# Attention with expert routing on one core: a new order of the first steps, the early gathers, expert 2's weights and the x stores

## The chip, the cores and the metric

The kernel runs on one core of one Trainium2 chip. The metric is the device time of one execution in microseconds (us); lower is better. The engines of the core work from queues of their own: TensorE (PE, its weight loads are PEld), VectorE (DVE), ScalarE (ACT), GpSimd (POOL) and SyncE (SP). POOL and SP, and in one place ACT, also issue the transfers (DMA).

## The reference

Attention over 8 batches of 8 heads, 576 rows of 64, with a causal mask in blocks of 64; then each of the 4608 rows of 512 goes through the expert that its domain id names.

```python
# _attn_ref(q, k, v): B, H, S, D = 8, 8, 576, 64
scores = (1.0 / np.sqrt(D)) * np.matmul(q, k.transpose(0, 1, 3, 2))
mask = block_i >= block_j                    # blocks of 64 rows
attn = softmax(np.where(mask, scores, -1e9))
x = (attn @ v).transpose(0, 2, 1, 3).reshape(B * S, H * D)   # 4608 x 512

# _moe_ref(x, domain_id, w1, w2): E = 8, w1 is E x 512 x 1024, w2 is E x 1024 x 512
for e in range(E):
    mask = domain_id == e
    h = np.maximum(x[mask] @ w1[e], 0.0)
    out[mask] = h @ w2[e]
```

## The kernel before

**Attention.** The work is cut into 32 steps (`npair`), four per batch; a step takes two heads. Each step `p` of the main loop (line 532) works on two pairs, and every engine takes its instructions in the order in which the loop writes them; no scheduler moves them.

- `emit_G0`, `emit_G1` and `emit_G2` (lines 384 to 405) form the scores of a pair on PE, in PSUM tiles `ps` (two buffers), and ACT takes their exponential into `A`: three exponentials of 128 x 1024 per pair.
- `emit_P` and `emit_D` multiply the previous pair's `A` by its `v` into `po`; `emit_N` lets DVE divide by the sums and write 16-bit rows into `x`.
- `emit_T(G, s)` lets PE transpose q (s = 0) or k (s = 1) of two pairs, group G, through the one PSUM tile `PT`, and DVE copies it to `QK`. The table `Ts` and `turn_qk` say at which point of which step this happens: (step, 0) at the start, (step, 1) behind `emit_G2`, (step, 2) behind the next pair's `G0`.
- `routing()` is a generator that works out, on DVE and with a few small matmuls (line 290), which row goes to which slot of which expert. Each step takes one portion of it (`next(rout, None)`), and step 24 takes the rest with `inv_mm` and `inv_close`, after which the table of row numbers `tok0` is known.

**Loads and stores.** POOL issues all loads: q, k and v of the batches in four buffers each (`qh`, `kh`, `vS`), a batch's v in five pieces by 128 rows, and the experts' weights in halves of w1 and w2 (`w1_half`, `w2_half`), which are converted from 32 to 16 bits on the way. A POOL transfer takes one of eight semaphores in turn, and so waits until the transfer eight before it has landed. `store_x` writes the normalised rows to the DRAM tensor `x_rows`: a small part (64 rows) and a large one (512 rows) per batch, for the last batch in two column parts, 0 to 320 behind step 31 and 320 to 512 behind step 32. SP issues them, but for the last large one, which ACT issues (line 449, `eng`).

**Experts.** Each expert has five blocks of 128 slots. A block's rows come from `x_rows` by an indirect transfer (a gather, line 468). The first three blocks of experts 0 and 1 hold rows of batches 0 to 4 only, so their gathers (`early_gather`, line 497, with a copy of the row numbers by `early_row`) are issued during the attention; the late ones (lines 679 to 682) wait for the last x store. `early_block` has PE transpose expert 0's first three blocks in steps 30 and 31. For the others DVE transposes (`turn`, line 618, 16 instructions), except blocks 3 and 4 of experts 0 and 1, which go through PE (`transpose_block`). `mm1` (line 635) forms the first product, ACT takes the positive part (line 639); `mm2` (line 648) forms the second, ACT copies it (line 654), and POOL scatters it to the output (line 655). Experts 0 and 1 are run in two parts: three early blocks of each, then two late blocks of each. The lists `todo` say between which scatters the next weight halves are issued.

**What sets the order around the change.** In steps 26 to 31 line 590 holds a written list: a number is a half of the weights of experts 1 and 2 (0 to 7), a negative number an early gather of expert 1. Weights 4 and 5, expert 2's w1, are issued in the last two steps, ahead of the late gathers; weights 6 and 7 lie between the first scatters.

## Time and profile before

| | us |
|---|---|
| three timed executions | 280.13, 285.47, 284.68 |
| their median | 284.68 |
| profiled execution, own time | 279.41 |
| profiled execution, span | 277.6 |

The span is what the profile covers, from the first instruction to the last; the execution's own time is 1.8 us longer. Busy time in the span: PE 248.0 us (89%), DVE 187.3 (67%), ACT 164.7 (59%), POOL 158.1 (57%). Such shares are averages over stages with different limits; what limits a stage is read from the waits in it. "[1.02 <-ACT hT L639]" behind a row of a timeline means that the engine sat idle for 1.02 us before it, and that the instruction of line 639 on ACT ended this. DMA share is the busy time of the core's 16 transfer engines; it can exceed 1, as packets overlap.

### The profile page before, as it was taken

The numbers are of one execution on the slowest core, as the hardware profiler recorded it, in microseconds if no ns is written. First come the engines' busy times: TensorE is split into PE (matmuls) and PEld (weight loads), VectorE is DVE, ScalarE is ACT, GpSimd is POOL, SyncE is SP. The second block draws the span as 40 slices with busy tenths as digits, with TensorE's granted clock in tenths as the row PEclk, the third lists the DMA queues.
The fourth block names the chain that finished last, engine by engine and source line by source line (L and its number), as shares of the span: only waits on it lengthen the run. The fifth ranks groups of instructions, "written<-read, shape, count | busy, mean of one in ns | idle before, by whom it ended". The sixth has DMA issues, their size and how long they took to land.

```text
span 277.6 us, 6942 instructions
## 1 busy us (share of the span) xinstructions
PE 248.0 (89%) x2878; PEld 154.9 (56%) x2878; DVE 187.3 (67%) x297; ACT 164.7 (59%) x218; POOL 158.1 (57%) x184
## 2 busy tenths in 40 slices
PE   8599799999999998891899989999999999999940
PEld 5366566666667665550456656474664656647510
DVE  4769899999997783329139919899495983960000
ACT  1658989999997899450335545364452644536420
POOL 8797473554635544305784888687778875151240
PEclk9989999999999999998699999999999999999985
DMA  6999999999999999994379989999899994121030
GB/s 86 158 153 176 222 192 209 197 212 189 224 194 213 196 231 253 243 239 98 103 162 239 258 234 198 271 186 259 193 223 275 192 266 173 63 109 61 38 135 2
DMA packets 65585, 50.85 MB, mean 183 GB/s; under 512 B 40973, under 2 KB 53773, under 8 KB 65552
## 3 DMA queue, kind: packets, MB, share of 16 engines
q0 software_dynamic: 59936, 45.63, 95.8%
q1 hardware_dynamic: 5088, 4.56, 6.1%
q8 instruction: 24, 0.39, 0.5%
q10 hardware_dynamic: 528, 0.20, 0.3%
q14 instruction: 9, 0.07, 0.1%
HBM read 67.15 MB, written 15.20 MB: 297 GB/s over the span
## 4 chain that ended last, share of the span: by engine, by line
PE 40%; DMA 19%; issue 15%; POOL 13%; DVE 4%; another core or an unknown queue 3%; ACT 2%; POOLq 1%; DVEq 0%; ACTq 0%
PE ps L373 8%; PE ph L635 7%; PE po L415 7%; DMA kh<-in_k_dram 7%; DMA out_dram<-osb,tok 7%; PE po L648 7%; POOL out_dram L655 5%; PE PT L362 5%; DMA xg<-x_rows,row 4%; PE po L426 4%; DVE xT L618 3%; POOL vS L94 2%; POOL xg L468 2%; PE ps L395 1%
## 5 line engine op out<-in xcount | busy, mean ns | idle before, releaser
L618 DVE STREAM_TRANSPOSE xT<-xg 32x640 f16<-32x640 f16 (+1 forms) x112 | 89.4, 798 | 28.5 <-DMA xg<-x_rows,tok 13.4
L378 ACT ACTIVATE A<-ps 128x1024 f16<-128x1024 f32 x96 | 92.1, 1024 | 13.1 <-PE ps L395 6.4
L635 PE MATMUL ph<-xT,w1h 128*128 128x320 f16 (+2 forms) x512 | 74.6, 303 | 9.3 <-DVE xT L618 6.9
L648 PE MATMUL po<-w2h,hT 128*128 128x512 f16 x320 | 71.2, 379 | 0.1
L639 ACT ACTIVATE hT<-ph 128x640 f16<-128x640 f32 (+2 forms) x80 | 47.5, 597 | 37.2 <-PE ph L635 29.6
L635 PEld LDWEIGHTS <-w1h 128*128 128x128 f16 x512 | 50.4, 99 | 33.4 <-issue 14.1
L655 POOL DMA_INDIRECT out_dram<-osb,tok x40 | 40.6, 1015 | 37.9 <-ACT osb L654 25.1
L648 PEld LDWEIGHTS <-hT 128*128 128x128 f16 x320 | 31.2, 98 | 36.1 <-issue 0.6
L654 ACT COPY osb<-po 128x512 f32<-128x512 f32 x40 | 23.4, 586 | 46.7 <-PE po L648 30.7
L468 POOL DMA_INDIRECT xg<-x_rows,tok x34 | 34.5, 1016 | 23.9 <-DMA x_rows<-x 13.3
L94 POOL DMA_DIRECT2D vS<-in_v_dram x40 | 33.2, 837 | 23.9 <-DMA kh<-in_k_dram 10.0
L365 DVE COPY QK<-PT 128x1152 f16<-128x1152 f16 x30 | 40.5, 1350 | 3.4 <-PE PT L362 2.4
L373 PE MATMUL ps<-QK 64*128 64x64 f16 (+3 forms) x320 | 39.2, 296 | 2.4 <-ACT A L378 0.8
L415 PE MATMUL po<-vS,A 128*128 128x65 f16 x640 | 29.8, 197 | 1.1 <-issue 0.4
L415 PEld LDWEIGHTS <-A 128*128 128x128 f16 x640 | 23.6, 99 | 10.4 <-issue 7.0
L439 DVE TENSOR_TENSOR x<-po,rc 128x640 f16<-128x640 f32 x32 | 26.4, 824 | 1.1
L426 PE MATMUL po<-vS,A 64*64 64x65 f16 (+1 forms) x320 | 21.0, 194 | 0.0
L373 PEld LDWEIGHTS <-QK 64*128 64x128 f16 x320 | 13.2, 94 | 7.4 <-issue 1.3
L426 PEld LDWEIGHTS <-A 64*64 64x64 f16 (+1 forms) x320 | 14.2, 106 | 1.9
L128 POOL DMA_DIRECT2D w2h<-in_moe_w_dram x16 | 12.2, 767 | 3.5 <-DMA kh<-in_k_dram 2.3
L123 POOL DMA_DIRECT2D w1h<-in_moe_w_dram x16 | 12.2, 767 | 3.2 <-DMA qh<-in_q_dram 1.9
L438 DVE RECIPROCAL rc<-po 128x10 f32<-128x10 f32 x32 | 7.0, 220 | 10.1 <-PE po L426 8.2
(102 smaller groups left out, 126.6 us busy)
## 6 DMA issues: line engine op xcount, KB each, us to landing
w1h<-in_moe_w_dram POOLq DMA_DIRECT2D x16, 512.0 KB
w2h<-in_moe_w_dram POOLq DMA_DIRECT2D x16, 512.0 KB
vS<-in_v_dram POOLq DMA_DIRECT2D x28, 128.0 KB
x_rows<-x SPq DMA_DIRECT2D x7, 512.0 KB, 9.6
qh<-in_q_dram POOLq DMA_DIRECT2D x6, 576.0 KB
kh<-in_k_dram POOLq DMA_DIRECT2D x6, 576.0 KB
vS<-in_v_dram POOLq DMA_DIRECT2D x16, 64.0 KB
qh<-in_q_dram POOLq DMA_DIRECT2D x3, 288.0 KB
```

Source lines behind the costliest of these rows:

```text
L94: nc.gpsimd.dma_start(out=vS[b % RV][r0:128, c, h0:h1, 16:80], in_=v[b, h0:h1, 128 * c : 128 * c + n, :].rearrange("h p d -> p h d"))
L365: nc.vector.tensor_copy(out=QKs[G][:, s].rearrange("p i (n j) -> p i n j", j=R), in_=P16.rearrange("p (j i n) -> p i n j", j=R, i=2))
L373: nc.tensor.matmul(out=o[:, t], lhsT=QK[h, 1, i, 128 * c : 128 * c + 128], rhs=QK[h, 0, i, q0:q1], start=True, stop=True)
L378: nc.scalar.activation(out=o, in_=i, func=AF.Exp, scale=0.125)
L415: nc.tensor.matmul(out=po[:, t, 65 * w : 65 * w + 65], lhsT=st["A"][:, t, n0 : n0 + 128], rhs=vS[b % RV][:, c, head(st, t), 15:80], start= ...
L426: nc.tensor.matmul(out=po[r0:128, t, 65 * w : 65 * w + 65], lhsT=st["A"][k : k + 64, t, n0 : n0 + 128 - r0], rhs=vS[b % RV][k : k + 64, c, ...
L468: nc.gpsimd.indirect_dma_start(out=g[:, blk, :], out_offset=None, in_=xd, in_offset=bass.IndirectOffsetOnAxis(ap=tok[:, 1, blk : blk + 1], ...
L618: nc.vector.transpose(out=dst[32 * j : 32 * j + 32, i, b0:b1], in_=src[32 * i : 32 * i + 32, j, b0:b1])
L635: nc.tensor.matmul(out=ph[:, i, 0:w], lhsT=w1_cols(w1h, dc, fc), rhs=xT[:, dc, c0 : c0 + w], start=(dc == 0), stop=(dc == 3))
L639: nc.scalar.activation(out=hT[:, fc, n0 : n0 + k * w].rearrange("p (i n) -> p i n", i=k), in_=ph[:, 0:k, 0:w], func=AF.Relu)
L648: nc.tensor.matmul(out=po[:], lhsT=hT[:, fc, 128 * blk : 128 * blk + 128], rhs=w2h[:, fc, :], start=(fc == 0), stop=(fc == 7))
L655: nc.gpsimd.indirect_dma_start(out=dst[blk], out_offset=bass.IndirectOffsetOnAxis(ap=tok[:, 0, blk : blk + 1], axis=0), in_=osb[:], in_off ...
```

## The change

It has five parts.

1. The early gathers of expert 1 are issued in the middle of steps 25, 26 and 27 (`mid_issue`), among those of expert 0, and stand ahead of expert 1's weights but for one half of w1. `early_row` becomes part of `early_gather`.
2. Weights in the loop are those of experts 0 and 1 alone (`late_issue`); expert 2's w1 is issued behind the late gathers of experts 0 and 1, ahead of expert 2's gathers.
3. `store_x` always uses SP, and the large part goes first.
4. In steps 0 and 1 the scores `G1` stand ahead of `turn_qk(p, 0)`; in step 2 the transpose of `turn_qk(2, 1)` stands behind the next pair's `G0`; the portion of the routing stands behind `turn_qk(p, 2)`.
5. Batch 1's first k load follows its first q load directly, and batch 1's v comes in ten pieces (four heads each) in place of five.

```diff
-    load_qk(1, 0, 2, (0,))
+    load_qk(1, 0, 2)
     load_v_chunks(0, 4, H, range(4))
-    load_qk(1, 0, 2, (1,))
     load_qk(1, 2, HP)
-    load_v_chunks(1, 0, H, range(5))
+    for h0 in (0, HP):
+        load_v_chunks(1, h0, h0 + HP, range(5))
...
-    def store_x(st, c0, c1, eng):
+    def store_x(st, c0, c1):
         b = st["p"] // HP
         x = st["x"]
-        nc.sync.dma_start(out=xd[S * b : S * b + 64, c0:c1], in_=x[64:128, 4, c0:c1])
-        eng.dma_start(
+        nc.sync.dma_start(
             out=xd[S * b + 64 : S * b + S, c0:c1].rearrange("(m p) d -> p m d", p=128),
             in_=x[:, 0:4, c0:c1])
+        nc.sync.dma_start(out=xd[S * b : S * b + 64, c0:c1], in_=x[64:128, 4, c0:c1])
...
+    mid_issue = {25: ((1, 0),), 26: ((1, 1),), 27: ((1, 2),)}
+    late_issue = {22: (0, 0), 24: ((0, 0), 0), 25: (0, (0, 1)), 26: (0, (0, 2)),
+                  27: (0,), 28: (0,), 29: (0,)}
...
-        turn_qk(p, 0)
         if p <= 1:
             emit_G1(st)
+        turn_qk(p, 0)
...
             emit_N(prev)
+            for g in mid_issue.get(p, ()):
+                early_gather(*g)
...
             emit_G2(st)
-            turn_qk(p, 1)
+            if p != 2:
+                turn_qk(p, 1)
...
+        if p == 2:
+            turn_qk(p, 1)
+        turn_qk(p, 2)
         next(rout, None)
-        turn_qk(p, 2)
...
-        for g in ((0,), (1, -1, 2), (-2, 3), (-3,), (4,), (5,))[p - 26] if 26 <= p < npair else ():
-            if g < 0:
-                early_gather(1, -1 - g)
+        for g in late_issue.get(p, ()):
+            if isinstance(g, int):
+                todo.pop(0)()
             else:
-                todo[g]()
+                early_gather(*g)
...
     for e in range(2):
         gather(xgs[e], tok_of(e), range(NE, NB))
+    todo = weights(2)
+    for f in todo[0:2]:
+        f()
     xgs[2] = new_xg()
     gather(xgs[2], tok_of(2), range(NB))
...
-    mm2(hT0, w2s[0], tok_of(0), dst_of(0), range(NE), todo[6:8])
+    mm2(hT0, w2s[0], tok_of(0), dst_of(0), range(NE), todo[2:4])
```

POOL's order from expert 0's third early gather to expert 2's gathers, before. `xg_2203` is expert 0's buffer, `xg_2204` expert 1's, `xg_2760` expert 2's; `w1h_2364` and `w2h_2365` are expert 1's weights, `w1h_2366` is expert 2's; `row02` is the row numbers of expert 0's third block.

```order
L499 DMA xg_2203<-x_rows,row02_2359 128x512
L123 DMA w1h_2364<-in_moe_w1_dram 128x2x1024 x2
L499 DMA xg_2204<-x_rows,row10_2368 128x512
L128 DMA w2h_2365<-in_moe_w2_dram 128x2x1024
L499 DMA xg_2204<-x_rows,row11_2370 128x512
L128 DMA w2h_2365<-in_moe_w2_dram 128x2x1024
L499 DMA xg_2204<-x_rows,row12_2372 128x512
L123 DMA w1h_2366<-in_moe_w1_dram 128x2x1024 x2
L468 DMA xg_2203<-x_rows,tok0_140 128x512 x2
L468 DMA xg_2204<-x_rows,tok0_140 128x512 x2
L468 DMA xg_2760<-x_rows,tok0_140 128x512 x5
```

The same stretch of POOL's order in the changed kernel: `xg_2174`, `xg_2175` and `xg_2765` are the buffers of experts 0, 1 and 2, `w1h_2209` and `w2h_2210` expert 1's weights, `w1h_2761` expert 2's.

```order
L494 DMA xg_2174<-x_rows,row01_2295 128x512
L494 DMA xg_2175<-x_rows,row11_2341 128x512
L123 DMA w1h_2209<-in_moe_w1_dram 128x2x1024
L494 DMA xg_2174<-x_rows,row02_2377 128x512
L494 DMA xg_2175<-x_rows,row12_2423 128x512
L123 DMA w1h_2209<-in_moe_w1_dram 128x2x1024
L128 DMA w2h_2210<-in_moe_w2_dram 128x2x1024 x2
L468 DMA xg_2174<-x_rows,tok0_145 128x512 x2
L468 DMA xg_2175<-x_rows,tok0_145 128x512 x2
L123 DMA w1h_2761<-in_moe_w1_dram 128x2x1024 x2
L468 DMA xg_2765<-x_rows,tok0_145 128x512 x5
```

Expert 1's three early gathers (`row10` two places ahead of this stretch, then `row11`, `row12`) moved ahead of its w2 and of the second half of its w1, expert 0's third one (`row02`) fell behind `row11` and half of w1, and expert 2's w1 moved behind the four late gathers.

ACT's order at the end of the attention, before: the last six exponentials (line 378), then the x store, then expert 0's first product.

```order
L378 ACTIVATE A_80<-ps 128x2x512 x3
L378 ACTIVATE A_81<-ps 128x2x512 x3
L449 DMA x_rows<-x 128x4x192
L639 ACTIVATE hT<-ph 128x384 x8
L654 COPY osb<-po 128x512 x3
```

The same place in the changed kernel (lines 636 and 651 are 639 and 654 of before).

```order
L378 ACTIVATE A_80<-ps 128x2x512 x3
L378 ACTIVATE A_81<-ps 128x2x512 x3
L636 ACTIVATE hT<-ph 128x384 x8
L651 COPY osb<-po 128x512 x3
L636 ACTIVATE hT<-ph 128x384 x8
```

The store left ACT's queue, so the positive part of expert 0's first product follows the last exponential directly.

DVE's order in steps 0 to 2, as a difference: line 365 is the copy of transposed q or k out of `PT`, lines 283 to 293 belong to the routing, lines 438 and 439 are `emit_N`.

```order
 L283 SCALAR_TENSOR_TENSOR inc<-msk,me 128x288
 L286 CAST mr<-inc 128x8
+L365 COPY QK<-PT 128x1152
 L291 COPY sc<-po 128x24
-L365 COPY QK<-PT 128x1152 x2
-L438 RECIPROCAL rc<-po 128x10
-L439 TENSOR_TENSOR x<-po,rc 128x2x5x64
+L365 COPY QK<-PT 128x1152
+L438 RECIPROCAL rc<-po 128x10
+L439 TENSOR_TENSOR x<-po,rc 128x2x5x64
+L365 COPY QK<-PT 128x1152
 L293 TENSOR_SCALAR off<-sc 128x8
```

The copies of transposed q and k moved ahead of the routing's portions: the first one ahead of line 291, the third one ahead of lines 293 to 302.

## Rows read from the trace of the kernel before

**Rows 1.** PE's timeline: start, busy us, instruction [idle before, what ended it].
```profile
116.40 4.24 PE L635 MATMUL ph<-xT,w1h 128*128 128x384 f16 x24 [1.02 <-ACT hT L639]
120.48 5.34 PE L648 MATMUL po<-w2h,hT 128*128 128x512 f16 x24
132.76 7.17 PE L635 MATMUL ph<-xT,w1h 128*128 128x384 f16 x32 [6.94 <-DVE xT L618]
...
179.74 8.85 PE L635 MATMUL ph<-xT,w1h 128*128 128x320 f16 x64
...
249.36 8.86 PE L635 MATMUL ph<-xT,w1h 128*128 128x320 f16 x64
```

**Rows 2.** Windows: length, busy us of each engine, PE clock, DMA share, GB/s.
```profile
115.00:120.00 5.00, 3.98 (x25) 2.14 (x23) 0.09 (x1) 2.84 (x6) 0.00 (x0) 1.00 1.11 242
...
126.00:128.00 2.00, 0.00 (x0) 0.00 (x0) 1.95 (x5) 0.44 (x1) 0.88 (x1) 1.00 0.46 88
...
130.00:135.00 5.00, 2.24 (x8) 1.09 (x9) 2.56 (x5) 0.49 (x1) 3.83 (x4) 0.50 0.35 105
...
145.00:150.00 5.00, 4.84 (x36) 3.32 (x35) 4.90 (x7) 2.84 (x8) 4.16 (x5) 1.00 1.05 253
...
155.00:160.00 5.00, 4.93 (x34) 3.23 (x34) 4.75 (x11) 2.71 (x8) 3.89 (x5) 1.00 1.09 263
```

**Rows 3.** DVE's timeline, end of attention and experts 1, 3 and 7.
```profile
114.26 0.82 DVE L439 TENSOR_TENSOR x<-po,rc 128x640 f16<-128x640 f32 x1
123.30 9.31 DVE L618 STREAM_TRANSPOSE xT<-xg 32x384 f16<-32x384 f16 x16 [8.22 <-DMA xg<-x_rows,row]
...
166.01 13.58 DVE L618 STREAM_TRANSPOSE xT<-xg 32x640 f16<-32x640 f16 x16 [5.38 <-PE ph L635]
...
233.76 13.58 DVE L618 STREAM_TRANSPOSE xT<-xg 32x640 f16<-32x640 f16 x16 [5.54 <-DMA xg<-x_rows,tok]
```

**Rows 4.** POOL's timeline, 111 to 163 us.
```profile
111.19 1.07 POOL L499 DMA_INDIRECT xg<-x_rows,row  x1 [0.30 <-issue]
112.27 1.57 POOL L123 DMA_DIRECT2D w1h<-in_moe_w_dram  x2
127.12 1.05 POOL L468 DMA_INDIRECT xg<-x_rows,tok  x1 [13.29 <-DMA x_rows<-x]
...
138.97 1.04 POOL L655 DMA_INDIRECT out_dram<-osb,tok  x1 [0.30 <-issue]
...
153.13 0.98 POOL L655 DMA_INDIRECT out_dram<-osb,tok  x1 [3.36 <-ACT osb L654]
...
162.60 1.00 POOL L468 DMA_INDIRECT xg<-x_rows,tok  x1 [0.30 <-issue]
```

**Rows 5.** Timeline of PE's weight loads, early blocks of expert 0.
```profile
108.64 0.23 PEld L482 LDWEIGHTS <-xg 128*128 128x128 f16 x4 [0.34 <-DMA xg<-x_rows,row]
...
112.16 0.21 PEld L482 LDWEIGHTS <-xg 128*128 128x128 f16 x3 [0.39 <-issue]
```

**Rows 6.** DMA issues: KB each, median us from issue to landing.
```profile
x_rows<-x SPq DMA_DIRECT2D x7, 64.0 KB, 5.5
x_rows<-x SPq DMA_DIRECT2D x1, 320.0 KB, 12.0
...
x_rows<-x ACTq DMA_DIRECT2D x1, 192.0 KB, 11.2
```

**Rows 7.** ACT's timeline, start of the attention.
```profile
15.60 1.02 ACT L378 ACTIVATE A<-ps 128x1024 f16<-128x1024 f32 x1 [3.32 <-PE ps L395]
```

**Rows 8.** PE's timeline, transposes of k.
```profile
13.65 1.17 PE L362 MATMUL PT<-identh,kh 128*64 128x128 f16 x18 [1.46 <-DVE QK L365]
...
34.44 0.69 PE L362 MATMUL PT<-identh,kh 128*64 128x128 f16 x18 [0.87 <-DMA kh<-in_k_dram]
```

**Rows 9.** POOL's timeline, loads of batches 1 and 2.
```profile
17.11 4.22 POOL L94 DMA_DIRECT2D vS<-in_v_dram  x5
...
22.04 0.79 POOL L75 DMA_DIRECT2D kh<-in_k_dram  x1
```

More of the change, by code (lines that the diff above doesn't have):

```diff
@@ L489, in early_block @@
                      xgs[0], xT, blk)
-    rows = {}
-    def early_row(e, w):
-        rows[e, w] = const.tile([128, 1], I32, name=f"row{e}{w}")
-        nc.vector.tensor_copy(out=rows[e, w][:], in_=tok_of(e)[:, 1, w : w + 1])
     def early_gather(e, w):
-        row = rows[e, w]
+        row = const.tile([128, 1], I32, name=f"row{e}{w}")
+        nc.vector.tensor_copy(out=row[:], in_=tok_of(e)[:, 1, w : w + 1])
         nc.gpsimd.indirect_dma_start(
@@ L555 @@
             emit_N(prev)
+            if p == 24:
+                xgs = {0: new_xg(), 1: new_xg()}
+                xT = new_xT()
+            for g in mid_issue.get(p, ()):
+                early_gather(*g)
             if prev["p"] == npair - 2:
-                store_x(prev, 0, DM - 192, nc.sync)
+                store_x(prev, 0, DM - 192)
             elif prev["p"] == npair - 1:
-                store_x(prev, DM - 192, DM, nc.scalar)
+                store_x(prev, DM - 192, DM)
             elif prev["p"] % HP == HP - 1:
-                store_x(prev, 0, DM, nc.sync)
+                store_x(prev, 0, DM)
         if st is not None:
             emit_G2(st)
-            turn_qk(p, 1)
+            if p != 2:
+                turn_qk(p, 1)
             if p >= npair - 2:
@@ L577 @@
         if p == 22:
-            for f in weights(0):
-                f()
+            todo = weights(0)
         if p == 24:
-            xgs = {0: new_xg(), 1: new_xg()}
-            xT = new_xT()
-        if 24 <= p < 24 + NE:
-            early_row(0, p - 24)
-            early_gather(0, p - 24)
-        if p == 26:
-            todo = weights(1) + weights(2)
-            for w in range(NE):
-                early_row(1, w)
-        for g in ((0,), (1, -1, 2), (-2, 3), (-3,), (4,), (5,))[p - 26] if 26 <= p < npair else ():
-            if g < 0:
-                early_gather(1, -1 - g)
+            todo += weights(1)
+        for g in late_issue.get(p, ()):
+            if isinstance(g, int):
+                todo.pop(0)()
             else:
-                todo[g]()
+                early_gather(*g)
         prev = st
```

## The prediction

> **What bounds the kernel now.** I read the windows first, then the timeline of TensorE (PE), and for each of its waits the timeline of the engine that ends it.
>
> Up to the last normalisation at 114.26 the attention runs [rows 3]; from 133 us on the experts run back to back. Between them lies the one large hole: PE ends expert 0's second product at 125.82 and idles 6.94 us until the transposes xT of expert 1 [rows 1]. Its granted clock is 0.50 in 130 to 135 [rows 2], so the 32 matmuls that follow take 7.17 us, where 24 of the same shape took 4.24, so 5.65 for 32: 1.5 us. With the 1.02 us that PE waited for ScalarE (ACT) at 116.40 [rows 1], whose queue held an x store until VectorE (DVE) had finished, the prize is at most 6.94 + 1.5 + 1.0 = 9.5 us.
>
> What ends the hole: DVE starts expert 1's 16 transposes at 123.30, after 8.22 us of waiting for a gather, and needs 9.31 us [rows 3]. That gather is the third early one of expert 1, issued by GpSimd (POOL) at 111.19 behind two halves of w2 [rows 4]. It lands 12 us after its issue because the queue is full: from 115 to 120 the DMA share is 1.11 at 242 GB/s. In 130 to 135 it is 0.35 at 105 GB/s, as POOL then only issues gathers, nine from 127.12 to 138.97, one per 1.3 us [rows 2, 4]. So the kernel is bound by transferred bytes up to about 126 us, by POOL's issue to about 139, by bytes again to about 165, and by PE after that.
>
> Behind the hole stands a second chain with no slack. POOL's late gathers start at 127.12, after 13.29 us of waiting for the last x store. In order on POOL follow five gathers of expert 2, eight scatters between six weight halves (the first at 138.97), and five gathers of expert 3, the last one at 162.60 [rows 4]. DVE's turn of expert 3 starts at 166.01 and takes 13.58 us [rows 3], to 179.59; PE comes for it at 179.74 [rows 1]. Expert 3 is the narrow place. For expert 7 there is room: its turn starts at 233.76 and ends at 247.34, PE comes at 249.36 [rows 1, 3].
>
> **The change part by part.**
> *Early gathers of expert 1 ahead of its weights.* The third one no longer stands behind w2. But expert 0's third gather, which PE transposes at 112.16 in the last attention step, now stands behind two gathers of expert 1 (0.13 MB each) and half of w1 (0.52 MB). Expert 0's first gather already came only just in time: LDWEIGHTS waited 0.34 us for it at 108.64 [rows 5]. The third follows 0.26 MB later, at about 109.8, and now another 0.79 MB later, 3.3 us at 242 GB/s: about 113.4. So PE stands about 1.3 us (bounds 0 and 4). Expert 1's third gather lands at about 114.5. With PE 1.3 us late the last normalisation, which ended at 115.08 [rows 3], ends at 116.4, and DVE turns expert 1 until 125.7. PE starts expert 0 at 115.2, has no ACT wait, and is through its two products 5.65 + 5.34 us later, at 126.2. No hole, no low clock: expert 1's first product ends at 131.9, not 139.9, and all that PE does behind it could come 8.0 us earlier, expert 3 at 171.7.
>
> *x stores by SP, the large part first.* This gives the 1.02 us just counted. The small part goes out behind it, which the landing of the large one hides.
>
> *Expert 2's w1 behind the late gathers.* Two halves of 0.52 MB leave the queue ahead of the last store: 1.05 MB at 242 GB/s are 4.4 us. The share of 126 to 128 is 0.46, between full and gathers alone [rows 2], so the queue ran dry at about 126.3, and now at about 121.9. The last store is issued at 116.4. Rows bound its landing: 5.5 us (median of the 64 KB stores) to 12.0 us (the 320 KB store) [rows 6], so 121.9 to 128.4. I take 122.5, just behind the dry queue, as the 192 KB store before (115.12 + 11.2 = 126.3) landed just there. POOL started 0.8 us after that, and starts now at 123.3, 3.8 us earlier. The two halves of w1 now cost POOL 1.57 + 0.3 us ahead of expert 2's gathers [rows 4], so the first scatter comes 13.7 us after the start, at 137.0 in place of 138.97. Expert 2's gathers are issued by 136.7, landed 2.4 us later, and turned at about 152.7; PE wants them one expert's pace of 17.4 us (179.74 to 249.36 for four) ahead of expert 3, at about 154.
>
> *The narrow place afterwards.* Up to expert 3's gathers POOL's work is the same. Its 3.36 us wait at 153.13 for a scatter's data goes, as PE is 8 us ahead; by POOL alone those gathers come 5.0 us earlier. But the bytes stay: shares are 1.05 in 145 to 150 and 1.09 in 155 to 160 [rows 2], the queue is full, and its work starts only 2.0 us earlier. So expert 3's turn comes 2.0 us (bytes) to 5.0 us (POOL) earlier. With shares above 1 I take 3.0, near the bytes: turn 163.0 to 176.6, PE at 176.7 in place of 179.74. PE, ready at 171.7, waits there 5 us: the hole moves from expert 1 to expert 3. Experts 4 to 7 keep their room, as the pace of 17.4 us is PE's.
>
> *Steps 0 to 2 and batch 1's loads.* ACT idles 3.32 us before its fifth exponential at 15.60 [rows 7], as PE transposes k of the next group at 13.65, behind a 1.46 us wait for DVE, ahead of the scores [rows 8]. With scores first it starts at about 12.9, 2.7 us ahead. But PE then waits for batch 2's k, which landed only at 34.4, 12.4 us after its issue at 22.04 [rows 8, 9]; that landing hangs on the bytes ahead of it, and these are the same. Ten v loads of half size in place of five (five took 4.22 us [rows 9]) put its issue at most 4.2 us later, behind a queue that is still several us deep; the landing moves by 0 to 1.5 us. Bounds: 2.7 us gained to 1.5 lost. I take nothing: the wait at 34.4 swallows the lead, and the late gathers follow the bytes anyway.
>
> Sum: 3.0 us, at the narrow place; the 9.5 us of the hole lie beside it. The profiled execution took 279.41 us (span 277.6, 1.8 around it), so 276.4. It is the lowest of the four times shown; these average 282.4, and the median of the three is 284.68. No row tells what separates them, so I set the forecast at the average: 279.4.
>
> **A rule against my value for the store.** The last stores landed 11.2 and 12.0 us after their issue, beside a full queue [rows 6]. The Trainium skill ("DMA: Bandwidth & Descriptors", section "Anatomy of one DMA") fits a transfer through the software queue as about 2.0 us plus bytes over 436 GB/s; for 192 KB that is an estimate of 2.5 us. By it the store lands at 118.9 and the first rival below holds in full. The rows speak against it as long as the queue is full, as it is at 116.4.
>
> **Rivals.**
> *A. The queue is no limit behind the attention.* Expert 3's gathers land 2.4 us after their last issue, as in the profile (163.6 to 166.0), and the store at its lower bound. For it: the share of 0.35 in 130 to 135, with room for all of w1. Against it: shares above 1 from 145 to 160. Time: 5.0 us by POOL, 0.6 by the store, and more if it lands sooner still, up to PE's 8.0: about 7 us, 275.4.
> *B. The lead of the start lives.* If batch 2's k lands by 31.7, the attention ends 2.7 us earlier. For it: batch 1's k is asked for earlier. Against it: the same bytes ahead of batch 2. 279.4 - 2.7 = 276.7.
> *C. Slower: the store keeps its 12.0 us.* Place: POOL's first late gather. Issued at 116.4 the store lands at 128.4, POOL starts at 129.2, and with the 1.87 us for w1 the first scatter is at 142.9, 3.9 us later than before; expert 3's turn starts 0.9 us (POOL) to 3.9 us (bytes) later. It decides from a landing at 124.5 on: from there the first scatter is later than before. For it: both large stores of this stretch took 11 us or more. Against it: 1.05 MB less stand in the queue. Time: 2.4 us on 282.4, 284.8.
> *D. The order does not do what it says.* If expert 1's third gather still lands after 117 (126.2 less the 9.31 us of DVE), a part of the hole stays; the narrow place hides the first 5 us of it. Beyond 122 nothing is gained: 282.4.
>
> **How the numbers follow.** Forecast 0.53, A 0.22, B 0.07, C 0.13, D 0.05. Range 273.5 to 286.0: below A by 2, as the lowest time shown is 3 under the average that it starts from; above C by 1, as the times shown reach 285.47. About 2% (5.6 us) is what a measurement of this kernel can tell from no change. Faster by more than that: most of A, and a little of B and of the forecast, 0.25. Slower by more: the far part of C, 0.08. Within: 0.67.
>
> **What would show it.** Right: no PE wait before expert 1's first product and a clock of 1.00 there; POOL's first late gather at 122 to 125; a PE wait of 3 to 7 us before expert 3's first product, ended by DVE's turn, whose gathers land late behind shares above 1; a PE wait near 112 for expert 0's third gather; a PE wait for batch 2's k near 34. Wrong: no wait of PE at expert 3 or a first late gather before 121 (then A), the attention ending before 111 (then B), a first scatter after 139 (then C).

## The result and the profile after

The changed kernel takes 282.72 us (median of 12 runs, 281.72 to 284.16) where the kernel before took 282.18 (median of 12, 280.13 to 286.68): ratio 1.0067, interval 1.0039 to 1.0096, so some 1.9 us slower where 3.0 us less were forecast. Ratios here leave disturbed executions out, and so need not equal the quotient of two medians (1.0019 here). The loss is under the 2% that the prediction named as what can be told from no change; that it is a loss rests on the interval. The profiled execution took 282.66 us (span 281.0).

PE's timeline of the changed kernel (start, busy us, instruction, idle before and what ended it) answers to [rows 1]:

```profile
115.86 0.40 PE L482 MATMUL ps<-identh,xg 128*128 128x128 f16 x4 [2.62 <-DMA xg<-x_rows,row]
117.34 7.24 PE L632 MATMUL ph<-xT,w1h 128*128 128x384 f16 x32
...
129.60 5.63 PE L632 MATMUL ph<-xT,w1h 128*128 128x384 f16 x32
...
180.62 11.48 PE L632 MATMUL ph<-xT,w1h 128*128 128x320 f16 x64 [6.17 <-DMA out_dram<-osb,tok]
```

The hole of 6.94 us before expert 1 is gone (129.60). Expert 3's first product starts at 180.62 instead of 179.74, after a wait of 6.17 us, and takes 11.48 us for 8.85. The profile names a scatter's landing as what ended the wait, but DVE's turn of expert 3 ends at 180.48 (166.90 + 13.58), 0.14 us before PE starts. Behind it no later first product of PE has a wait of its own, so what is late here is late at the end.

DVE's and POOL's timelines of the same kernel answer to [rows 3] and [rows 4]:

```profile
117.71 0.82 DVE L439 TENSOR_TENSOR x<-po,rc 128x640 f16<-128x640 f32 x1
118.45 9.30 DVE L615 STREAM_TRANSPOSE xT<-xg 32x384 f16<-32x384 f16 x16
...
166.90 13.58 DVE L615 STREAM_TRANSPOSE xT<-xg 32x640 f16<-32x640 f16 x16 [8.61 <-DMA xg<-x_rows,tok]
```

```profile
126.77 1.08 POOL L468 DMA_INDIRECT xg<-x_rows,tok  x1 [14.57 <-DMA x_rows<-x]
...
140.31 1.04 POOL L652 DMA_INDIRECT out_dram<-osb,tok  x1 [0.30 <-ACT osb L651]
...
160.92 1.00 POOL L468 DMA_INDIRECT xg<-x_rows,tok  x1 [0.30 <-issue]
```

DVE turns expert 1 directly behind the last normalisation. The first late gather starts at 126.77 (before 127.12), the first scatter 13.54 us later, and DVE waits for expert 3's gathers, the last issued at 160.92, until 166.90. The windows (length, busy us of each engine, PE clock, DMA share, GB/s) show both ends of the attention, where [rows 2] stood:

```profile
25.00:30.00 5.00, 5.00 (x106) 3.53 (x106) 4.79 (x9) 4.58 (x5) 5.00 (x7) 1.00 1.15 130
118.00:120.00 2.00, 2.00 (x8) 0.99 (x7) 1.97 (x4) 0.72 (x2) 0.00 (x0) 0.50 1.14 230
...
126.00:127.00 1.00, 1.00 (x6) 0.42 (x5) 0.98 (x2) 0.59 (x1) 0.23 (x1) 1.00 0.00 0
...
180.00:185.00 5.00, 4.38 (x17) 2.57 (x18) 4.04 (x6) 0.70 (x1) 4.00 (x5) 0.50 0.97 184
```

From 126 to 127 the queues are empty: POOL's late gathers come behind the last byte of the last store. The clock is 0.50 behind both waits of PE, at 118 and at 180. And from 25 to 30 the queues move 130 GB/s while POOL (fifth pair of numbers) is busy for 5.00 of 5.00 us: there the loss shows first, as the experiments will tell. POOL's busy time alone does not tell it, as the same stretch of the kernel before has POOL at 4.81 with 200 GB/s:

```profile
25.00:30.00 5.00, 5.00 (x102) 3.42 (x100) 4.61 (x7) 4.74 (x6) 4.81 (x6) 1.00 1.47 200
```

PE's wait for batch 2's k and the large last stores (KB, us to landing) answer to [rows 8] and [rows 6]:

```profile
35.76 0.69 PE L362 MATMUL PT<-identh,kh 128*64 128x128 f16 x18 [0.90 <-DMA kh<-in_k_dram]
```

```profile
x_rows<-x SPq DMA_DIRECT2D x1, 320.0 KB, 11.1
x_rows<-x SPq DMA_DIRECT2D x1, 192.0 KB, 7.1
```

### The profile page after: what moved, and what is told of

It reads as the page before. It is cut to its first block, busy times and chain, and to the rows that moved or that the text cites. A ratio compares the mean times of both kernels' runs of the same rounds, so it can differ in the third digit from the quotient of the medians.

```text
span 281.0 us, 6945 instructions
## 1 busy us (share of the span) xinstructions
PE 253.6 (90%) x2878; PEld 157.8 (56%) x2878; DVE 186.5 (66%) x297; ACT 164.8 (59%) x218; POOL 161.9 (58%) x189
## 4 chain that ended last, share of the span: by engine, by line
DMA 35%; PE 32%; POOL 15%; issue 14%; ACT 1%; POOLq 1%; ACTq 0%
PE ph L632 14%; DMA kh<-in_k_dram 11%; PE po L645 10%; DMA out_dram<-osb,tok 6%; POOL out_dram L652 5%; DMA vS<-in_v_dram 5%; POOL vS L94 5%; DMA w1h<-in_moe_w_dram 5%; DMA w2h<-in_moe_w_dram 4%; DMA xg<-x_rows,row 4%; PE po L415 2%; PE ps L373 2%; PE PT L362 2%; POOL xg L468 1%; PE po L426 1%
## 5 line engine op out<-in xcount | busy, mean ns | idle before, releaser
L632 PE MATMUL ph<-xT,w1h 128*128 128x320 f16 (+2 forms) x512 | 77.2, 310 | 6.9 <-DMA out_dram<-osb,tok 6.2
L632 PEld LDWEIGHTS <-w1h 128*128 128x128 f16 x512 | 51.5, 101 | 32.4 <-DMA out_dram<-osb,tok 6.6
L94 POOL DMA_DIRECT2D vS<-in_v_dram x45 | 36.5, 826 | 22.6 <-DMA vS<-in_v_dram 8.7
L373 PE MATMUL ps<-QK 64*128 64x64 f16 (+3 forms) x320 | 40.6, 305 | 2.8 <-ACT A L378 2.0
L426 PE MATMUL po<-vS,A 64*64 64x65 f16 (+1 forms) x320 | 21.8, 197 | 0.1
L123 POOL DMA_DIRECT2D w1h<-in_moe_w_dram x16 | 12.3, 774 | 4.9 <-DMA qh<-in_q_dram 1.7
```

The source lines that it names most:

```text
L94: nc.gpsimd.dma_start(out=vS[b % RV][r0:128, c, h0:h1, 16:80], in_=v[b, h0:h1, 128 * c : 128 * c + n, :].rearrange("h p d -> p h d"))
L373: nc.tensor.matmul(out=o[:, t], lhsT=QK[h, 1, i, 128 * c : 128 * c + 128], rhs=QK[h, 0, i, q0:q1], start=True, stop=True)
L426: nc.tensor.matmul(out=po[r0:128, t, 65 * w : 65 * w + 65], lhsT=st["A"][k : k + 64, t, n0 : n0 + 128 - r0], rhs=vS[b % RV][k : k + 64, c, ...
L632: nc.tensor.matmul(out=ph[:, i, 0:w], lhsT=w1_cols(w1h, dc, fc), rhs=xT[:, dc, c0 : c0 + w], start=(dc == 0), stop=(dc == 3))
```

## Experiments

The theory was that expert 3 is the narrow place and that all edits act through the start of the first late gather. Its rivals were that the front of the kernel, the transferred bytes, or the hole itself sets the end. Ratios are to the kernel before, timed beside each.

| run | edit | ratio (interval) | first late gather | expert 3's turn |
|---|---|---|---|---|
| after | all parts | 1.0067 (1.0039 to 1.0096) | 126.77 | 166.90 |
| a_v5 | after, v in 5 pieces | 0.9939 (0.9903 to 0.9976) | 123.53 | 163.41 |
| a_qk2 | after, batch 2's q, k between the halves of v | 1.0030 (0.9983 to 1.0077) | - | - |
| b_v10 | before, v in 10 pieces | 1.0125 (1.0035 to 1.0216) | 130.37 | 170.18 |
| b_order | parts 1 to 3 | 0.9985 (0.9943 to 1.0026) | 126.27 | 166.24 |
| b_g02 | parts 1 to 3, third gather ahead | 0.9908 (0.9867 to 0.9949) | 125.85 | 166.27 |
| b_w1 | part 2's w1 of expert 2 alone | 0.9965 (0.9924 to 1.0006) | 123.59 | 166.56 |
| b_early | parts 1 and 3 | 1.0105 (1.0029 to 1.0182) | 129.96 | 168.50 |
| b_gath | part 1 | 0.9977 (0.9925 to 1.0028) | 128.52 | 166.95 |
| a_best1, a_best5 | after, 5 pieces, third gather and expert 3's gathers ahead | 0.9837 (0.9736 to 0.9938), 0.9891 (0.9832 to 0.9949) | 124.66, 123.99 | 159.48, 158.50 |

In the first five kernels of the table with both times, expert 3's turn starts 39.8 to 40.4 us behind the first late gather; 39.7 had been forecast (163.0 - 123.3). In b_early and b_gath it is 38.5 and 38.4, in b_w1 43.0.

**v in five pieces again** (a_v5).

```diff
-    for h0 in (0, HP):
-        load_v_chunks(1, h0, h0 + HP, range(5))
+    load_v_chunks(1, 0, H, range(5))
```

> The changed kernel with batch 1's v in five pieces again. Narrow-place theory: the ten pieces left the queue short of work from 25 to 30 us (130 GB/s against 200 in the kernel before), so batch 2's k landed 1.3 us later and everything counted in bytes with it; five pieces give back 1.0 to 1.5 us: k awaited until about 34.4, turn of expert 3 near 165.6, ratio 1.001 to 1.003. Rival (the late k comes from the order of steps 0 to 2 and PE's clock of 0.50 there): k still lands near 35.7 and the ratio stays at 1.007.

Measured: 279.57 us, 0.9939, 1.3% under the changed kernel, some 3.6 us; the expected gain was 1.0 to 1.5. Three kernels with ten pieces timed beside it took 283.4 (a_g02), 282.74 (a_deep3) and 281.85 us (a_fill). The forecast's places are hit: first late gather 123.53, expert 3's turn 163.41, PE there at 177.13. The window of 25 to 30 us of this kernel, and PE at expert 3:

```profile
25.00:30.00 5.00, 5.00 (x108) 3.52 (x104) 4.78 (x9) 4.74 (x6) 3.31 (x5) 1.00 1.30 206
```

```profile
177.13 10.82 PE L631 MATMUL ph<-xT,w1h 128*128 128x320 f16 x64 [4.88 <-DMA out_dram<-osb,tok]
```

POOL is busy for 3.31 us and waits for landings; 206 GB/s move instead of 130. So the split, and not the order of the end, carries the loss. POOL's timeline, first of the changed kernel, then of a_v5, shows what the split does:

```profile
17.52 5.10 POOL L94 DMA_DIRECT2D vS<-in_v_dram  x7
22.80 2.10 POOL L94 DMA_DIRECT2D vS<-in_v_dram  x3 [0.17 <-issue]
24.89 0.75 POOL L75 DMA_DIRECT2D qh<-in_q_dram  x1
```

```profile
17.17 4.24 POOL L94 DMA_DIRECT2D vS<-in_v_dram  x5
21.33 0.82 POOL L75 DMA_DIRECT2D qh<-in_q_dram  x1
...
25.33 0.88 POOL L94 DMA_DIRECT2D vS<-in_v_dram  x1 [0.68 <-DMA vS<-in_v_dram]
...
29.90 0.74 POOL L75 DMA_DIRECT2D kh<-in_k_dram  x1 [1.05 <-DMA qh<-in_q_dram]
```

With five pieces POOL runs ahead and has to wait until earlier loads have landed (2.01, then 1.15 us in the kernel before). With ten it issues from 15 us on and waits for no landing until 31.3: its issuing sets the pace. Batch 1's v is 0.59 MB, so 7.20 us of issuing are 82 GB/s and 4.24 us are 139 (an estimate from these rows).

**Ten pieces on the kernel before** (b_v10), the same edit backwards.

> The kernel before with one edit: batch 1's v in ten pieces of four heads. Theory (the ten pieces leave the queue short of work in 25 to 30 us and delay batch 2's k, and all that follows the bytes): DMA share of 25 to 30 falls from 1.47 towards 1.15, PE's wait for batch 2's k grows from 0.87 by 1 us or more, POOL's first late gather moves from 127.1 to 128.5 or later, time 283.7 to 286.0 (1.3 to 3.6 above 282.4). Rival (the ten pieces cost only where the scores stand first): no later landing, 282.4 within 0.6. My forecast's own value for this term was 0 to 1.5 with 0 taken.

Measured: 284.02 us, 1.0125; the theory holds. The same window, and PE at batch 2's q:

```profile
25.00:30.00 5.00, 4.85 (x99) 3.21 (x95) 4.57 (x8) 4.74 (x6) 5.00 (x7) 1.00 1.16 101
```

```profile
32.78 0.69 PE L363 MATMUL PT<-identh,qh 128*64 128x128 f16 x18 [2.93 <-DMA qh<-in_q_dram]
```

POOL is again busy throughout, 101 GB/s move (200 before), and PE waits 2.93 us for batch 2's q, where the trace of before shows 0.58 (at 30.72). Here POOL also waits twice, 0.68 and 0.70 us, until the load eight before has landed, in the middle of the pieces. The first late gather comes 3.25 us later than before. The interval is wide, as there are four executions.

**Where the loss goes** can be read from the same four traces. Windows from the start to 30 us and from there to 115, first of the changed kernel and a_v5, then of b_v10 and the kernel before:

```profile
0.00:30.00 30.00, 25.98 (x399) 17.77 (x400) 19.40 (x48) 16.20 (x17) 26.42 (x42) 0.77 1.29 138
30.00:115.00 85.00, 80.30 (x1604) 54.95 (x1599) 73.33 (x121) 77.51 (x82) 41.67 (x50) 1.00 1.50 212
```

```profile
0.00:30.00 30.00, 25.62 (x402) 17.91 (x402) 19.70 (x48) 16.36 (x18) 24.87 (x39) 0.83 1.35 153
30.00:115.00 85.00, 80.40 (x1605) 55.43 (x1602) 73.18 (x121) 76.61 (x82) 39.84 (x48) 1.00 1.50 214
```

```profile
0.00:30.00 30.00, 24.72 (x428) 17.31 (x428) 21.68 (x51) 18.06 (x19) 25.13 (x40) 0.94 1.26 130
30.00:115.00 85.00, 80.40 (x1568) 55.20 (x1569) 70.46 (x117) 74.50 (x79) 42.23 (x52) 0.96 1.50 211
```

```profile
0.00:30.00 30.00, 24.36 (x428) 17.20 (x428) 21.67 (x50) 17.78 (x19) 24.79 (x38) 0.94 1.34 148
30.00:115.00 85.00, 81.17 (x1613) 55.88 (x1610) 72.97 (x122) 76.26 (x80) 41.32 (x50) 1.00 1.50 213
```

In the first 30 us ten pieces move 15 and 18 GB/s less, 0.45 and 0.54 MB. In the 85 us behind, all four move 211 to 214 GB/s on average, and 167 or more in every 5 us, so the bytes are never made up: at 115 us 0.62 and 0.71 MB are missing, at 240 GB/s 2.6 to 3.0 us (an estimate), of the 3.24 and 3.25 us by which the late gather moves. The end of the attention does not set it: a_fill (below), which has the changed kernel's front, ended its attention 3.3 us later in its profiled execution, and its late gather came no later than 126.77:

```profile
121.01 0.82 DVE L439 TENSOR_TENSOR x<-po,rc 128x640 f16<-128x640 f32 x1
```

```profile
126.52 1.07 POOL L468 DMA_INDIRECT xg<-x_rows,tok  x1 [15.38 <-DMA x_rows<-x]
```

**Batch 2's q and k between the halves of v** (a_qk2).

```diff
-    for h0 in (0, HP):
-        load_v_chunks(1, h0, h0 + HP, range(5))
+    load_v_chunks(1, 0, HP, range(5))
     load_qk(2, 0, HP)
+    load_v_chunks(1, HP, H, range(5))
```

> The changed kernel with batch 2's q and k loads between the two halves of batch 1's v, which stays in ten pieces. Theory (the ten pieces hurt through POOL's later issue of what stands behind them: qh and kh of batch 2 were issued at 24.9 and 25.6 instead of 21.3 and 22.0): PE does not wait for batch 2's k, which is now behind five pieces only, first late gather at 124 to 125.5, 279.5 to 281. Rival (small pieces keep the queue short of work wherever they stand: 101 to 130 GB/s in 25 to 30 us in all five kernels with ten pieces, 178 to 207 with five): GB/s of 20 to 30 stays low, the first late gather at 126.5 to 127.5, 282 to 283.

Measured: 282.01 us, 1.0030; nearer the rival, with an interval that overlaps that of the changed kernel. Only the time is used of this run. Saving these two loads alone does not bring the 3.6 us back. The ten pieces still cost POOL the same issuing, only later, which would explain it; that is argued and not shown.

**Parts 1 to 3 on the kernel before** (b_order): the start as before, v in five pieces.

> The changed kernel with parts 4 and 5 undone (start as before, five pieces of v), so before plus parts 1 to 3: early gathers, expert 2's w1 and the x stores. Theory (the narrow place at expert 3, as forecast): no PE wait before expert 1's first product, first late gather near 123.5, DVE's turn of expert 3 near 163, PE waits 4 to 6 us at expert 3 and runs there at the lower clock for a while, 279.4 to 280.4. Rival (the gain of the run with five pieces came from the new start, the order of the end is worth nothing): 281.8 to 282.6.

Measured: 280.81 us, 0.9985, between the two. Expert 1 runs without a hole and PE waits 5.44 us at expert 3, as the theory says, but the first late gather comes at 126.27, not near 123.5. PE had waited 2.71 us for expert 0's third gather, and its product took 7.44 us behind it. By the windows this execution also had moved only 22.3 MB by 115 us, 0.5 MB less than a_v5, with 105 GB/s from 15 to 20 us; why, stays open.

**Expert 0's third gather ahead of half of w1**, on the changed kernel (a_g02), on parts 1 to 3 (b_g02), and with five pieces (a_v5g02).

```diff
-    late_issue = {22: (0, 0), 24: ((0, 0), 0), 25: (0, (0, 1)), 26: (0, (0, 2)),
+    late_issue = {22: (0, 0), 24: ((0, 0), 0), 25: (0, (0, 1)), 26: ((0, 2), 0),
```

> The changed kernel with expert 0's third early gather one place earlier, ahead of the half of w1. Narrow-place theory (the end follows DVE's turn of expert 3, which follows the last x store and the transfers behind it): PE's 2.6 us wait near 113 goes to under 0.6 us, the last store is issued 2.3 us earlier, but lands only 1.5 to 2 us earlier as the queue is still busy; the turn of expert 3 starts near 165, PE waits there 8 to 9 us in place of 6.2, and the time falls by 1 to 2 us: ratio to the kernel before 1.000 to 1.003. Rival (what the front loses reaches the end whole): 2.6 us of wait and 1.6 us of low clock behind it come off, ratio 0.992.

> The kernel before plus parts 1 to 3 as in the run without parts 4 and 5 (280.81 us, last store issued 119.08, PE waited 2.71 us for expert 0's third early gather), with that gather ahead of half of w1. Theory (the place of this gather costs the chain its wait and a stretch of low clock, some 2.7 + 1.8 us, which the last store and the late gathers hand on to expert 3): no such wait, last store near 116, first late gather near 124, expert 3's first product 2 to 3 us earlier, 277.9 to 279.2; the forecast for parts 1 to 3 had been 279.4. Rival (bytes alone set the narrow place, the front's loss is hidden): 280.5 to 281.1.

> The changed kernel with batch 1's v in five pieces and expert 0's third early gather ahead of half of w1. With five pieces alone it took 279.57 us and PE did not wait for that gather, but the attention ended later (early block at 114.67). Theory (both costs are one chain): 277.8 to 279.4, PE waits 4 to 6 us at expert 3. Rival (the five pieces already give all there is): 279.4 to 280.2. Beside the run with the old start it shows whether the new order of steps 0 to 2 is worth anything: equal within 0.6 us if the wait for batch 2's k swallows it, 1 to 2 us less if it lives.

Measured: 283.4 us (1.0044, 1.0000 to 1.0089), 280.67 (0.9908, 0.9867 to 0.9949) and 280.17 (0.9940, 0.9900 to 0.9980). In all three PE's wait is gone and expert 0's first product takes 5.64 us instead of 7.24 (in a_v5 PE had no such wait either). In a_g02 and a_v5g02 the ratio does not move beyond its interval. On parts 1 to 3 it falls by 0.0077, beside intervals that overlap slightly, but the times themselves, 280.81 (b_order) and 280.67 us, and PE at expert 3, first of b_order, then of b_g02, hardly differ:

```profile
179.97 10.41 PE L629 MATMUL ph<-xT,w1h 128*128 128x320 f16 x64 [5.44 <-DMA out_dram<-osb,tok]
```

```profile
180.00 10.35 PE L629 MATMUL ph<-xT,w1h 128*128 128x320 f16 x64 [3.99 <-DMA out_dram<-osb,tok]
```

The fall comes from the kernel before, which was timed anew beside each. So no run shows that the place of this gather reaches the end; that b_g02's gain over before, 2.6 us, is near the 3.0 forecast can be luck. Beside b_g02, a_v5g02 shows the new order of steps 0 to 2: 0.9940 for 0.9908, no gain.

**Expert 2's w1 alone behind the late gathers**, on the kernel before (b_w1).

```diff
-        for g in ((0,), (1, -1, 2), (-2, 3), (-3,), (4,), (5,))[p - 26] if 26 <= p < npair else ():
+        for g in ((0,), (1, -1, 2), (-2, 3), (-3,), (), ())[p - 26] if 26 <= p < npair else ():
...
         gather(xgs[e], tok_of(e), range(NE, NB))
+    for f in todo[4:6]:
+        f()
```

> The kernel before with one edit: expert 2's two halves of w1 behind the late gathers of experts 0 and 1 instead of in the last two steps. Theory (the last store lands when the queue has run dry, and 1.05 MB less are 4.4 us): first late gather at 122.5 to 125 instead of 127.1, expert 3's turn 40 us behind it, at 162.5 to 165; PE, held up by the hole before expert 1, is itself not ready for expert 3 before 179, so the time stays at 281.5 to 283. Rival (the store's landing hangs on its own issue, not on the queue): first late gather at 126.5 to 127.5, and with POOL's 1.87 us for the halves a time of 283 to 285.

Measured: 279.89 us, 0.9965. The first late gather at 123.59 confirms the forecast's 123.3; expert 3's turn at 166.56 was a miss. PE and POOL of this kernel:

```profile
131.16 7.86 PE L635 MATMUL ph<-xT,w1h 128*128 128x384 f16 x32 [4.12 <-DVE xT L618]
```

```profile
123.59 1.03 POOL L468 DMA_INDIRECT xg<-x_rows,tok  x1 [12.78 <-DMA x_rows<-x]
...
151.84 0.98 POOL L655 DMA_INDIRECT out_dram<-osb,tok  x1 [4.08 <-ACT osb L654]
```

The hole before expert 1 still holds PE, so POOL waits 4.08 us at 151.84 for a scatter's data (3.36 in the kernel before) and loses its lead. Part 2 without part 1 is swallowed by the hole.

**Parts 1 and 3 without part 2** (b_early), **and part 1 alone** (b_gath): expert 2's w1 stays in steps 30 and 31; b_gath also has the stores of before.

```diff
-                  27: (0,), 28: (0,), 29: (0,)}
+                  27: (0,), 28: (0,), 29: (0,), 30: (0,), 31: (0,)}
...
-            todo += weights(1)
+            todo += weights(1) + weights(2)
...
-    todo = weights(2)
-    for f in todo[0:2]:
-        f()
```

> The kernel before with the new order of the early gathers and the x stores by SP, but expert 2's w1 still ahead of the late gathers (in steps 30 and 31) and the start as before. Theory (40 us from the first late gather to expert 3's turn, less the 1.87 us for the halves): the hole before expert 1 is gone, the first late gather comes no earlier than 127, expert 3's turn at 165.5 to 167.5, PE waits 4 to 6 us there and is slow for 2 us behind it: 281.5 to 283.5, no gain, though 7 us of idle time are gone from expert 1. Rival (the hole was the bound): 276 to 279.

> The kernel before with the new order of the early gathers alone: expert 2's w1 still in steps 30 and 31, stores as before (small part first, the last large one by ACT). Theory (the store's move to SP cost the landing): first late gather at 126.5 to 128 instead of 129.96, no empty stretch of the queues ahead of it, expert 3's turn at 165 to 167, 281 to 282 on a kernel of 280.3 to 282.4 before, 1 to 2.5 us below the run with SP's stores. Rival (the order of gathers and weights moved the bytes): first late gather at 129 to 130.5, time as that run, 1.01 of before.

Measured: 283.81 us (1.0105) and 282.9 (0.9977). PE's timeline of b_early:

```profile
125.96 5.63 PE L629 MATMUL ph<-xT,w1h 128*128 128x384 f16 x32
...
182.23 11.34 PE L629 MATMUL ph<-xT,w1h 128*128 128x320 f16 x64 [7.26 <-DMA out_dram<-osb,tok]
```

Expert 1 starts 6.8 us earlier than before, without a wait, and the kernel is slower: the hole was not the bound. The two intervals just miss each other (1.0029 and 1.0028), from two sessions, so with w1 in front the store's move to SP may cost up to 1%; more is not shown. The 192 KB store (KB, us to landing), first of b_early, then of b_gath:

```profile
x_rows<-x SPq DMA_DIRECT2D x1, 192.0 KB, 12.3
```

```profile
x_rows<-x ACTq DMA_DIRECT2D x1, 192.0 KB, 11.1
```

That is 1.2 us of landing, and the late gather comes 1.44 us earlier; b_gath's 128.52 lies between the theory's 126.5 to 128 and the rival's 129 to 130.5, so each has a part.

**The clock held ahead of expert 3** (a_fill): 26 matmuls whose result nobody reads stand before its first product.

```diff
+    def hold_clock(n, w):
+        pd = new_po()
+        for _ in range(n):
+            nc.tensor.matmul(out=pd[:], lhsT=w[:, 0, 0:128], rhs=w[:, 0, :],
+                             start=True, stop=True)
...
+        if e == 3:
+            hold_clock(26, w2s[2])
         mm1(xT, hT, w1s[e])
```

> The changed kernel with 26 matmuls of 512 columns into an unused PSUM tile between expert 2 and expert 3; they add work and change nothing of the result. They fill 5.6 us of PE's 6.2 us wait. If the low clock behind the wait costs what its rows say (11.48 us for 64 matmuls in place of 8.86), the time falls by 2 to 2.6 us, ratio 0.998 to 1.000, with a clock of 1.00 in expert 3. If the end does not hang on PE behind the turn of expert 3, it stays at 1.007 or rises.

Measured: 281.85 us, 1.0006 (0.9946 to 1.0066). PE's timeline:

```profile
176.14 5.78 PE L676 MATMUL po<-w2h 128*128 128x512 f16 x26
181.75 8.86 PE L632 MATMUL ph<-xT,w1h 128*128 128x320 f16 x64
```

The product takes 8.86 us instead of 11.48, as expected. The time moves the same way, but within the intervals.

**Expert 3's gathers earlier**: ahead of expert 1's early scatters (a_deep3), or only ahead of expert 0's two late ones, with five pieces and the third gather ahead (a_best1, again as a_best5, and b_best2 with the start of before). The second move, without the other two edits:

```diff
     turn(xgs[2], xT2, 0, NB)
+    xgs[3] = new_xg()
+    gather(xgs[3], tok_of(3), range(NB))
     mm1(xT0, hT0, w1s[0], ((CE, CAP - CE),))
...
     mm1(xT1, hT1, w1s[1], ((CE, CAP - CE),))
-    xgs[3] = new_xg()
-    gather(xgs[3], tok_of(3), range(NB))
```

> The changed kernel with expert 3's five gathers issued ahead of the scatters of expert 1's first part. Narrow-place theory: they land by 156, DVE turns expert 3 directly behind expert 2 (from 158.4 to 172), PE finds it ready at 174.5; the 6.2 us wait and 2.6 us of low clock behind it go, expert 4's turn (from about 181, to 195) becomes the narrow place with a PE wait of 2 to 4 us: time 4 to 7 us less, ratio 0.983 to 0.993. Rival (the bytes alone set the time, the order only moves the wait): what is moved behind comes late instead, ratio 1.004 to 1.010.

> The changed kernel with three edits: batch 1's v in five pieces, expert 0's third early gather ahead of half of w1, and expert 3's five gathers issued ahead of the two late scatters of expert 0 and the two weight halves between them, instead of behind. Theory (POOL's issue order sets the narrow place): the gathers start some 4 us earlier (2 x 1.3 for scatters, 2 x 0.8 for halves), DVE's turn of expert 3 at 159 to 160, PE's wait there falls from 4.9 to about 1 us and its low clock with it, 274.5 to 276.5. Rival (transferred bytes set it): the two halves only change places with 0.65 MB of gathers, the turn comes at most 1 to 2 us earlier and expert 4 or expert 2 waits instead, 278 to 279.5.

> The same three edits with the start of the kernel before (parts 4 and 5 undone). Theory (start and end are independent, and the start's new order is swallowed by the wait for batch 2's k): within 0.6 us of the run with the new start and five pieces. Rival (the new order of steps 0 to 2 is worth something once the ten pieces are gone): 1 to 2 us slower than that run.

> The kernel of 276.46 us once more, in five rounds (five pieces of v, expert 0's third early gather ahead of half of w1, expert 3's gathers ahead of expert 0's late scatters). Theory: 0.980 to 0.988 of before. Rival (the four runs of the first time were lucky): 0.99 or more.

Measured: a_deep3 282.74 us (1.0034, 0.9991 to 1.0076), a miss. It has no wait at expert 3, but PE waits for ACT in expert 1's second part, so that expert 2 starts at 163.17 (156.70 in the changed kernel), and a little at expert 4, whose turn DVE starts only at 185.20. That the scatters hold ACT's output copies, as the rival of a_best4 has it, is not shown:

```profile
156.34 1.01 PE L632 MATMUL ph<-xT,w1h 128*128 128x256 f16 x4 [1.54 <-ACT hT L636]
...
198.92 8.85 PE L632 MATMUL ph<-xT,w1h 128*128 128x320 f16 x64 [0.94 <-issue]
```

The milder move is the fastest version that was measured twice: a_best1 276.46 us (0.9837), a_best5 277.78 (0.9891), b_best2 277.61 (0.9889, 0.9798 to 0.9981), each faster than both kernels. a_best1's PE:

```profile
154.54 10.53 PE L631 MATMUL ph<-xT,w1h 128*128 128x320 f16 x64 [3.55 <-DVE xT L614]
...
173.53 8.86 PE L631 MATMUL ph<-xT,w1h 128*128 128x320 f16 x64
...
193.93 8.86 PE L631 MATMUL ph<-xT,w1h 128*128 128x320 f16 x64 [2.91 <-DVE xT L614]
```

PE does not wait at expert 3 any more, but at experts 2 and 4 (193.93 is expert 4's product; the expectations of the next two runs call it expert 5's). Expert 3's turn comes 3.9 to 4.9 us earlier than in a_v5, where the rival allowed 1 to 2, so POOL's order sets the narrow place more than the bytes do; that the wait moves to experts 2 and 4 is what the rival said. The old start in b_best2 is within the intervals of the new one.

**Two more moves of POOL's order** on a_best1: expert 2's w1 behind its own gathers (a_best3), and expert 4's gathers earlier as well (a_best4).

```diff
     todo = weights(2)
-    for f in todo[0:2]:
-        f()
     xgs[2] = new_xg()
     gather(xgs[2], tok_of(2), range(NB))
+    for f in todo[0:2]:
+        f()
...
     mm1(xT1, hT1, w1s[1], ((CE, CAP - CE),))
+    xgs[4] = new_xg()
+    gather(xgs[4], tok_of(4), range(NB))
...
-        if e + 2 < E:
+        if 4 < e + 2 < E:
```

> The 276.46 us kernel (five pieces, third early gather ahead of half of w1, expert 3's gathers ahead of the late scatters of expert 0) with expert 2's two halves of w1 behind its gathers instead of ahead. There PE waited 3.55 us at expert 2 (DVE's turn started at 140.81, 6.26 us late, and the clock was low for 1.7 us more) and 2.91 at expert 5. Theory (POOL's order: 1.87 us of issue and 1.05 MB leave the path of expert 2's gathers): the turn starts 2 to 5 us earlier, PE waits 0 to 1 us at expert 2; part of it comes back at expert 3 to 5: 273.0 to 275.0. Rival (the bytes are only exchanged and expert 3 or 4 waits the longer): 276 to 277.5.

> The same with expert 4's five gathers ahead of expert 1's two late scatters and four weight halves, instead of behind. Theory: DVE's turn of expert 4 started at 180.20 after 7.14 us of waiting for them, so it can come 4 to 6 us earlier, and PE's 2.91 us at expert 5 go: 1.5 to 3 us less than the run beside it. Rival (the weights that now stand behind come late instead, scatters hold ACT's output buffers): same or slower than the run beside it.

Measured: a_best3 281.34 us (0.9828, 0.9712 to 0.9945), no better than a_best1 or a_best5. Expert 2's turn comes 2.85 us earlier than in a_best1, as expected, and PE waits 3.50 us at expert 3 instead: the rival. a_best4 gave a median of 281.6 us from four executions and no ratio; it stays open.

**The stores of before in a_best1** (a_best6).

```diff
-                store_x(prev, DM - 192, DM)
+                store_x(prev, DM - 192, DM, nc.scalar)
```

> The fastest kernel so far (277.0 span, 0.989 and 0.984 of before in two measurements) with the stores as before. Theory (ACT's queue of its own lets the last store land earlier): first late gather at 121.5 to 123.5 instead of 124.0 to 124.7; PE waits 1 us for ACT at expert 0, which PE's later waits hide; 1 to 2 us less, 0.977 to 0.985 of before. Rival (SP's queue costs nothing, ACT's 1 us is lost): 0.985 to 0.995.

Measured: 281.09 us, 0.9900 (0.9831 to 0.9969), as a_best5. The attention ended late in its profiled execution, the store left ACT at 119.84 into an almost empty queue, and landed quickly. In b_g02, where the attention also ended late, the same store by SP did so too (second line):

```profile
x_rows<-x ACTq DMA_DIRECT2D x1, 192.0 KB, 2.8
```

```profile
x_rows<-x SPq DMA_DIRECT2D x1, 192.0 KB, 2.7
```

Where little stands ahead of the store, SP's queue costs nothing that can be measured. The Trainium skill ("DMA: Bandwidth & Descriptors", section "Anatomy of one DMA") fits transfers that GpSimd issues as about 2.0 us plus bytes over 436 GB/s, an estimate of 2.5 us for this size. These stores are SP's and ACT's, so the fit is not for them, though the prediction used it so; 2.7 and 2.8 us lie near it, the 7.1 us of the changed kernel do not.

## Why the prediction was wrong

**What bounds the kernel, the hole, the narrow place: right.** The hole went and brought nothing by itself (b_early, b_gath); PE's wait moved to expert 3, 6.17 us for the 5 forecast, ended by DVE's turn behind shares above 1. From the late gather to the first scatter 13.54 us passed for 13.7, to the turn 40.1 for 39.7, from there to PE 13.72 for 13.7.

**The step that failed: the cost of batch 1's loads.** It was put at nothing ("I take nothing") for two reasons: the wait at 34.4 swallows the lead, and "the late gathers follow the bytes anyway", which were taken to be the same. Two runs in opposite directions put the ten pieces at 1.3% each: some 3.6 us taken away (a_v5), some 3.5 us added (b_v10). The bound of this step even held: batch 2's q was issued 3.6 us later (24.89 for 21.29; 4.2 had been named), and batch 2's k was transposed 1.32 us later (35.76 for 34.44; 0 to 1.5 had been named). The late gathers do follow the bytes, but the bytes were late: POOL issues for 7.20 us what it issued in 4.24, the queues have moved 0.45 MB less by 30 us than with five pieces, they run at nearly the same rate from there to 115 us, and the first late gather comes 3.24 us later (126.77 for 123.53). A loss at the front is paid in full at the end, because the queues never run dry in between; the wait of PE at 34.4 has no part in it.

The Trainium skill ("Perfetto Trace Analysis") has both sides. Its section "DMA Optimizations" says that splitting transfers may let work start sooner while the DMA engines are idle; their share here is 1.29 to 1.35 in the first 30 us. Its section "What 'DMA-bound' means" counts an issuing engine that is solid with DMA slices as a bound of its own. By the windows POOL is busy for 14.83 of the 15 us from 15 to 30 in the changed kernel and for 12.96 in a_v5, so the trace agrees with the second.

**Expert 0's third gather: right in kind, too small, and not on the path.** PE stood 2.62 us for the forecast 1.3 (bounds 0 and 4). The sum also left out that the clock falls behind such a wait: 7.24 us for 5.64, another 1.6. The last store was issued at 118.56, not 116.4. But the late gather does not hang on it: without the wait it comes at 127.29 (a_g02), and with an attention that ends 3.3 us later at 126.52 (a_fill).

**The x stores by SP: a gain counted, a cost left out.** ACT's 1.02 us went as forecast, but PE waits at expert 3 anyway. With two halves of w1 ahead of it the store's new queue may cost up to 1% (b_early beside b_gath); without them nothing is seen (a_best6).

**Expert 2's w1: right.** Alone it moves the first late gather to 123.59 (forecast 123.3); in the changed kernel the ten pieces take that back, to 126.77.

**The low clock behind the moved hole: not in the sum.** The forecast moved the hole, took its 1.5 us of low clock away at expert 1 and put none at expert 3. There the product took 2.6 us longer; in a_fill, with PE kept busy up to it, it took 8.86, so this is the clock. With the late gather 3.5 us late and PE slow for 2.6, the forecast's 276.4 on the profile becomes 282.5; 282.66 was measured.

**The lead of the start** did not live: the fifth exponential starts at 13.92 (before 15.60), the sixth at 18.20 (before 17.67). Runs with the old start and with the new one do not differ in one direction.

**Rivals.** C's sign came true by another mechanism: the large stores landed in 11.1 and 7.1 us, not 12, and its first scatter behind 139 (140.31) came from the later start. A failed on both points: the shares stay above 1, and the stores are slow. B and D did not happen. Why a_qk2 did not undo the ten pieces' loss stays open.

## What to carry to other kernels

Look for the narrow place behind the wait that you remove, and add there what the moved wait brings with it, a stretch of low clock above all. When a load is split, ask whether the issuing engine still waits for landings: while it does, it is ahead of the queues; once it does not, its issuing sets the pace, and pieces that cost nearly as much to issue as the whole slow everything behind them. Follow an early edit through every load behind it, by the bytes moved up to a given time, since bytes lost near the start reach the end through queues that never run dry.
